# Attention scores from keys and queries split into a rounded part and a rest, three products instead of one fp32 matmul

## The chip, the cores and the metric

One core of a Trainium2 chip runs the whole program. The metric is the device time of one execution in microseconds; lower is better.

## The reference

The program computes an attention layer with a compressive memory, a mixture of experts with hard routing, and a dense mixture of experts with Sinkhorn weights. Only the attention is touched here. Cut to it:

```python
B, H, S, D = 4, 8, 576, 64
scores = (q @ k.T) / sqrt(D)              # causal mask, per batch and head
a = softmax(scores)                       # max taken off, sum + 1e-9
local = a @ v
q_p = where(q > 0, q, exp(q) - 1) + 1     # phi
mem = (q_p @ M_prev) / (q_p . z_prev + 1e-6)
out = g * mem + (1 - g) * local           # g = sigmoid(beta), per head
# out goes, as rows of 512, into the two mixtures of experts
```

All inputs and outputs are fp32.

## The kernel before

The attention works in 16 units (the function `attention`, variable `u`): a unit is one batch and one pair of heads, and the two heads lie in partitions 0 to 63 and 64 to 127 once they are transposed. Per unit the 576 tokens are four tiles of 128 and one of 64.

For unit `u` the kernel loads k, q, v (`load`, on SP's queue), works out phi on ScalarE, GpSimd and VectorE (`phi_a`, `phi_b`, `phi_c`), and transposes k, q and phi on TensorE into PSUM (`trans`, parts 0, 1, 2 for the first 512 tokens, 3 for the last 64 of all). The transposed keys leave PSUM by a VectorE copy (line 204), the queries half by ScalarE (line 206) and half by VectorE (line 207), times 0.125, and phi by ScalarE (line 209, tile `pT`). The last 64 tokens leave by lines 211 to 215.

`score(u, i)` makes the scores of query tile `i` against `w` keys. For `i` from 0 to 3 there is one fp32 matmul for each head, 64 rows deep (line 233), and a bf16 matmul that adds the mask (line 235); then VectorE takes the maximum of both heads (line 237, tile `nm`), and ScalarE the exponentials with their sums, head by head (line 239, tile `P`). Tile 4 holds the last 64 queries of both heads side by side, 128 rows deep, in two matmuls of 288 keys (line 243), with lines 244 to 247 behind it.

`ptrans(u, k)` transposes the probabilities back on TensorE (lines 268, 276, 283, 289) and takes them out of PSUM into `pt`, for `k` in `DVE_PT` on VectorE, else on ScalarE (lines 270, 279); `k` = 6 is shared by both (lines 285, 286). `inverse` transposes the reciprocal sums (lines 173, 174). `av(u, part)` multiplies phi with the memory (line 298, which reads `pT`) and the probabilities with v (line 306) in one PSUM tile, called `x` here, and VectorE scales it into `xT` (line 307). Every fourth unit the router is run on a finished batch (`rt.batch`).

The stage is software-pipelined: the body for `u` runs the scores of unit `u`, the `ptrans` and `av` of unit `u` - 1 and the `trans` of unit `u` + 1, in five steps. The scores come in the order 3, 2, 1, 0, 4; after score 3 come `ptrans` 5 and 4 and `trans` part 0 (keys); after score 2 `ptrans` 0 and 1, `inverse` and part 1 (queries); after score 1 `ptrans` 2 and 3 and part 2 (phi); after score 0 `ptrans` 6 and 7, the first half of `av` and part 3; after score 4 the second half of `av`.

PSUM has two score tiles (`ps_s`, two banks each) and four others of one bank (`ps_t`), which the transposes, the `x` tiles and the router share: a tile is written again only when what reads it is done. Each engine works its own queue in order. The order of each queue in this stage is set when the kernel is built, by a planner that starts from the program's order and takes an instruction that it holds to be ready before one that it doesn't. The two mixtures behind the attention have their order written by hand, and already use matmuls of three products on tiles of type fp32r, split by a ScalarE copy (the rounded part) and a VectorE subtraction (the rest).

Of the kernel before, what the change touches and what calls it, by code (L numbers as in the profile page):

```python
# [9 lines left out]
F32 = mybir.dt.float32  # L10
F32R = mybir.dt.float32r
BF16 = mybir.dt.bfloat16
I32 = mybir.dt.int32
AF = mybir.ActivationFunctionType
ALU = mybir.AluOpType
# [3 lines left out]
B, H, S, D = 4, 8, 576, 64  # L19
# [2 lines left out]
DM = H * D  # L22
NT = 5
DVE_PT = (1, 3, 5)
TW = [128, 128, 128, 128, 64]


def attention(ctx, tc, q, k, v, M_prev, z_prev, beta, xT, ident, router=None):
    nc = tc.nc
    es = ctx  # L30
    c1 = es.enter_context(tc.tile_pool(name="at_c", bufs=1))
    nat = es.enter_context(tc.tile_pool(name="at_nat", bufs=3))
    tmp = es.enter_context(tc.tile_pool(name="at_tmp", bufs=2))
    tr = es.enter_context(tc.tile_pool(name="at_tr", bufs=2))
# [38 lines left out]

    qTp = []
    for i in range(2):
        t = c1.tile([128, 640], F32, name=f"qTp{i}")
        nc.gpsimd.memset(t[:, 512:], 0.0)
        qTp.append(t)
    Mb = []
    for i in range(2):  # L80
        t = c1.tile([128, NP, 128], F32, name=f"Mb{i}")
# [3 lines left out]
    zt, ld, ph, un = {}, {}, {}, {}  # L85

    nrm, Rs = [], []
    for i in range(2):
        t = c1.tile([128, NT, 2], F32, name=f"nrm{i}")
        nc.vector.memset(t, 1.0)  # L90
        nrm.append(t)
        t = c1.tile([128, S], F32, name=f"R{i}")
# [83 lines left out]
    def phi_t(u):  # L176
        if "pT" not in un[u]:
            un[u]["pT"] = tr.tile([128, S], F32, tag="pT", name="pT")
        return un[u]["pT"]

    def trans(u, part):


        qt = qTp[u % 2]
        p = ps_t.tile([128, 512], F32, tag="t", name="tp")
        if part == 0:
            un[u] = {"kT": tr.tile([128, S], F32, tag="kT", name="kT"), "P": {}}
        if part < 3:
            src = (ld.get((u, "k")), ld.get((u, "q")), ph[u][1] if u in ph else None)[part]
            for i in range(4):  # L190
                nc.tensor.transpose(p[:, i * 128:(i + 1) * 128], src[:, i], ident)
        else:
            src = []
            if part == 3:
                src += [ld[u, "k"], ld[u, "q"]]
                if u > 0:
                    src.append(ph[u - 1][1])
            else:
                src += [ph[u][1]]
            for n, t in enumerate(src):  # L200
                nc.tensor.transpose(p[:, n * 64:(n + 1) * 64], t[:64, 4], ident[:64, :64])

        if part == 0:
            nc.vector.tensor_copy(un[u]["kT"][:, :512], p)
        elif part == 1:
            nc.scalar.activation(qt[:, 256:512], p[:, 256:], AF.Copy, scale=0.125)
            nc.vector.tensor_scalar(qt[:, :256], p[:, :256], 0.125, None, ALU.mult)
        elif part == 2:
            nc.scalar.copy(phi_t(u)[:, :512], p)
        elif part == 3:  # L210
            nc.vector.tensor_copy(un[u]["kT"][:, 512:], p[:, 0:64])
            nc.scalar.activation(qt[0:64, 512:576], p[0:64, 64:128], AF.Copy, scale=0.125)
            nc.vector.tensor_scalar(qt[64:128, 576:640], p[64:128, 64:128], 0.125, None, ALU.mult)
            if u > 0:
                nc.vector.tensor_copy(phi_t(u - 1)[:, 512:], p[:, 128:192])
        else:
            nc.vector.tensor_copy(phi_t(u)[:, 512:], p[:, 0:64])

    def score(u, i):

        b, a = divmod(u, NP)
        kT = un[u]["kT"]
        qt = qTp[u % 2]
        s = ps_s.tile([128, 2, 512], F32, tag="s", name="s")
        nm = sm.tile([128, 2], F32, tag="nm", name="nm")
        if i == 3:
            un[u]["su"] = sm.tile([128, NT, 2], F32, tag="su", name="su", bufs=2)
        sums = un[u]["su"][:, i]
        if i < 4:
            w = (i + 1) * 128  # L230
            for h in range(2):
                r = slice(h * 64, (h + 1) * 64)
                nc.tensor.matmul(s[:, h, :w], qt[r, i * 128:(i + 1) * 128], kT[r, :w], start=True, stop=False)
            for h in range(2):
                nc.tensor.matmul(s[:, h, w - 128:w], idb, mk, start=False, stop=True)
            P = pp.tile([128, 2, w], F32, tag=f"P{i}", name=f"P{i}")
            nc.vector.tensor_reduce(nm, s[:, :, :w], AX.X, ALU.max, negate=True)
            for h in range(2):
                nc.scalar.activation(P[:, h], s[:, h, :w], AF.Exp, bias=nm[:, h:h + 1], accum_out=sums[:, h:h + 1])
        else:  # L240
            w = 288
            for h in range(2):
                nc.tensor.matmul(s[:, h, :w], qt[:, 512:640], kT[:, h * w:(h + 1) * w], start=True, stop=(h == 0))
            nc.tensor.matmul(s[:, 1, 224:288], idb, mk2, start=False, stop=True)
            P = pp.tile([128, 2, w], F32, tag=f"P{i}", name=f"P{i}")
            nc.vector.tensor_reduce(nm[:, 0:1], s[:, :, :w], AX.XY, ALU.max, negate=True)
            nc.scalar.activation(P, s[:, :, :w], AF.Exp, bias=nm[:, 0:1], accum_out=sums[:, 0:1])
        un[u]["P"][i] = P
# [8 lines left out]
    def ptrans(u, k):  # L257
# [7 lines left out]
        if k < 4:  # L265
            j, h = divmod(k, 2)
            for i in range(j, 4):
                nc.tensor.transpose(p[:, (i - j) * 128:(i - j + 1) * 128], P[i][:, h, j * 128:(j + 1) * 128], ident)
            ev = nc.vector.tensor_copy if k in DVE_PT else nc.scalar.copy
            ev(pt[:, h, j, j * 128:512], p[:, :512 - j * 128])  # L270
        elif k < 6:
            j = k - 2
            n = 4 - j
            for h in range(2):
                for i in range(j, 4):
                    nc.tensor.transpose(p[:, (h * n + i - j) * 128:(h * n + i - j + 1) * 128],
                                        P[i][:, h, j * 128:(j + 1) * 128], ident)
            ev = nc.vector.tensor_copy if k in DVE_PT else nc.scalar.copy
            ev(pt[:, :, j, j * 128:512], p[:, :2 * n * 128].rearrange("p (h q) -> p h q", h=2))
# [12 lines left out]
    def av(u, part):  # L292
# [7 lines left out]
        for j in range(nj):  # L300
            for h in range(2):
                kk = TW[j]
                lv = vn[:kk, j, h * 64:(h + 1) * 64]
# [13 lines left out]
    for part in (0, 1, 3):  # L317
        trans(0, part)
    phi_a(0)
    for u in range(NU + 1):  # L320
# [9 lines left out]
        for n in range(5):  # L330
            if sc:
                score(u, (3, 2, 1, 0, 4)[n])
                if n == 4:
                    phi_c(u)
            if ex:
                if n == 0:
                    norm(u - 1)
                    ptrans(u - 1, 5)
                    ptrans(u - 1, 4)
                elif n < 3:  # L340
                    ptrans(u - 1, 2 * n - 2)
                    ptrans(u - 1, 2 * n - 1)
                    if n == 1:
                        inverse(u - 1)
                    else:
                        trans(u - 1, 2)
                elif n == 3:
                    ptrans(u - 1, 6)
                    ptrans(u - 1, 7)
                    av(u - 1, 0)  # L350
                else:
                    av(u - 1, 1)
                    if rt and u % NP == 0:
                        rt.batch(u // NP - 1, ps_t)
            if sc:
                if n == 0:
                    phi_b(u)
                elif n == 2:
                    gate_v(u)
                elif n == 3 and u + 1 == NU:  # L360
                    trans(u, 4)
# [290 lines left out]
def tile_attention_moe_moe(ctx, tc, q, k, v, M_prev, z_prev, beta, modality_id, w_gate1, modality_bias, w1a, w2a,  # L652
# [10 lines left out]
    with ExitStack() as actx:  # L663
        xTp = actx.enter_context(tc.tile_pool(name="xTp", bufs=1))
        xT = xTp.tile([128, NP, N], F32, name="xT")
        rt = attention(actx, tc, q, k, v, M_prev, z_prev, beta, xT, ident,
                       lambda: Router(actx, tc, c, xT, ident, modality_id, w_gate1, modality_bias))
        rt.table(rt.ps)
        rt.busy(64)
# [618 lines left out]
```

## Time and profile before

| what | us |
|---|---|
| three runs | 2077.13, 2078.49, 2080.11 (median 2078.49) |
| the profiled execution | 2078.23 |
| its span | 2076.5 |
| busy TensorE, VectorE, ScalarE, GpSimd over the span | 2038.2, 1480.6, 853.7, 776.9 |
| the attention's 16 units, first score to the end of the last unit's scores | about 11 to 266 |

The profile is of one execution. PE is TensorE, PEld its weight loads, DVE VectorE, ACT ScalarE, POOL GpSimd, SP the engine that issues most DMAs. A wait is put down to the instruction that ended it.

### The profile page before, as it was taken

Reading aid. Unit: us, or ns where it says so; the run is one execution under the profiler, and the core shown is the slowest. Engines: PE = TensorE matmul, PEld = TensorE weight load, DVE = VectorE, ACT = ScalarE, POOL = GpSimd, SP = SyncE. Lnnn points to the kernel's source line nnn. Section 1 sums busy time; section 2 is a strip of 40 time slices with the busy share of each in tenths; the row PEclk is TensorE's granted clock in tenths of the full one; section 3 lists DMA queues with packets and bytes.
Section 4 is the critical chain, followed back from the end, with each engine's and each line's share of the span. In section 5 each row is a group of like instructions: output and inputs, shape, how many; then the busy total and the mean of one; then the engine's idle time right before and its main releaser. Section 6 shows DMA issues by size and latency. Waiting matters only on the chain.

```text
span 2076.5 us, 31532 instructions
## 1 busy us (share of the span) xinstructions
PE 2038.2 (98%) x11528; PEld 1768.1 (85%) x11528; DVE 1480.6 (71%) x2573; ACT 853.7 (41%) x1808; POOL 776.9 (37%) x800
## 2 busy tenths in 40 slices
PE   7999999999899999999999999999999999999998
PEld 4666669999698998998888999899888899899987
DVE  6788757666786776667786677777678676677775
ACT  4656536555634333333343333333334433333332
POOL 6666511000133344344454334334355333333332
PEclk9999999999999999999999999999999999999999
DMA  7332146665611233444432222222223222122221
GB/s 189 83 75 78 33 153 229 202 210 170 215 51 61 68 67 69 62 66 77 61 107 67 61 77 66 62 76 67 62 62 111 62 63 80 61 64 79 62 62 40
DMA packets 238520, 187.35 MB, mean 90 GB/s; under 512 B 71440, under 2 KB 194320, under 8 KB 238352
## 3 DMA queue, kind: packets, MB, share of 16 engines
q1 hardware_dynamic: 229008, 171.48, 30.2%
q0 software_dynamic: 3520, 9.46, 1.3%
q10 hardware_dynamic: 5824, 4.25, 0.7%
q8 instruction: 95, 1.56, 0.3%
q14 instruction: 73, 0.60, 0.1%
HBM read 171.51 MB, written 13.64 MB: 89 GB/s over the span
## 4 chain that ended last, share of the span: by engine, by line
PE 46%; issue 16%; POOL 8%; DVE 3%; ACT 1%; POOLq 0%; DVEq 0%; ACTq 0%
PE y L1092 24%; PE prod L1021 21%; POOL T L913 4%; POOL w1l L907 3%; DVE w2l L907 0%; DVE c L1035 0%; DVE u L1035 0%; POOL out_dram L394 0%; DVE hl L1044 0%; PE lq L1133 0%; DVE S2l L907 0%; ACT hh L1039 0%; DVE A11l L907 0%; DVE A12l L907 0%; DVE csum L1166 0%
## 5 line engine op out<-in xcount | busy, mean ns | idle before, releaser
L1039 ACT ACTIVATE hh<-c 128x384 fp32r<-128x384 f32 x384 | 202.0, 526 | 837.3 <-DVE c L1035 837.2
L907 POOL TENSOR_TENSOR w1l<-T,w1h 128x1024 fp32r<-128x1024 f32 x94 | 226.7, 2412 | 851.0 <-ACT w1h L907 851.0
L1092 PE MATMUL y<-w2h,hh 128*128 128x512 f32 x1152 | 453.8, 394 | 0.0
L1092 PE MATMUL y<-w2l,hh 128*128 128x512 f32 x1152 | 453.8, 394 | 0.0
L1092 PE MATMUL y<-w2h,hl 128*128 128x512 f32 x1152 | 453.0, 393 | 0.0
L1044 DVE SCALAR_TENSOR_TENSOR hl<-c,hh 128x384 fp32r<-128x384 f32 x384 | 415.4, 1099 | 1.4 <-ACT hh L1039 1.0
L1035 DVE TENSOR_TENSOR c<-prod,u 128x384 f32<-128x384 f32 x288 | 160.3, 557 | 157.2 <-PE prod L1021 156.7
L1092 PEld LDWEIGHTS y<-w2h,hh 128*128 128x128 f32 x1152 | 216.5, 188 | 32.7
L1092 PEld LDWEIGHTS y<-w2h,hl 128*128 128x128 f32 x1152 | 216.5, 188 | 28.3
L1092 PEld LDWEIGHTS y<-w2l,hh 128*128 128x128 f32 x1152 | 216.7, 188 | 27.8
L913 POOL TENSOR_TENSOR T<-r,T 128x256 f32<-128x256 f32 x188 | 157.8, 840 | 14.1 <-issue 7.0
L913 POOL TENSOR_TENSOR T<-r 128x256 f32<-128x256 f32 x188 | 158.8, 845 | 7.1
L1035 DVE TENSOR_TENSOR u<-prod,u 128x384 f32<-128x384 f32 x192 | 106.0, 552 | 58.3 <-PE prod L1021 58.0
L1035 DVE TENSOR_TENSOR u<-prod,p 128x384 f32<-128x384 f32 x96 | 53.5, 557 | 127.2 <-PE prod L1021 127.1
L907 DVE TENSOR_TENSOR w2l<-r,w2h 128x512 fp32r<-128x512 f32 x188 | 137.1, 729 | 0.5 <-ACT w2h L907 0.5
L907 ACT CAST w2h<-r 128x512 fp32r<-128x512 f32 x188 | 106.7, 610 | 0.0
L907 DVE TENSOR_TENSOR w1l<-r,w1h 128x512 fp32r<-128x512 f32 (+1 forms) x188 | 104.6, 557 | 0.0
L1035 DVE TENSOR_TENSOR c<-prod,p 128x384 f32<-128x384 f32 x96 | 53.4, 557 | 68.8 <-PE prod L1021 64.1
L907 ACT CAST w1h<-T 128x1024 fp32r<-128x1024 f32 x94 | 97.0, 1032 | 1.0 <-POOL T L913 1.0
L1049 ACT COPY p<-prod 128x384 f32<-128x384 f32 x96 | 46.1, 480 | 120.8 <-PE prod L1021 120.6
L1103 DVE SCALAR_TENSOR_TENSOR acc<-y,P,acc 128x512 f32<-128x512 f32 x126 | 92.5, 744 | 4.3 <-PE y L1092 4.3
L907 ACT CAST w1h<-r 128x512 fp32r<-128x512 f32 (+1 forms) x188 | 94.5, 503 | 0.0
(386 smaller groups left out, 4202.9 us busy)
## 6 DMA issues: line engine op xcount, KB each, us to landing
r<-in_moe_w_dram SPq DMA_DIRECT2D x188, 512.0 KB, 4.5
r<-in_moe_w_dram SPq DMA_DIRECT2D x188, 256.0 KB, 2.9
xr<-xs_sorted SPq DMA_DIRECT2D x22, 256.0 KB, 5.1
kn<-in_k_dram SPq DMA_DIRECT2D x32, 128.0 KB, 2.6
qn<-in_q_dram SPq DMA_DIRECT2D x32, 128.0 KB, 2.7
vn<-in_v_dram SPq DMA_DIRECT2D x32, 128.0 KB, 2.8
xs_sorted<-zrow ACTq DMA_DIRECT2D x16, 256.0 KB, 3.1
zb<-in_z_prev_dram SPq DMA_DIRECT2D x4, 256.0 KB, 3.8
```

The costliest lines, as they stand in the source:

```text
L907: return (lambda: nc.scalar.copy(hi, src)), (lambda: eng.tensor_tensor(lo, src, hi.bitcast(F32), ALU.subtract))
L913: sub = lambda i, a, b: (lambda: nc.gpsimd.tensor_tensor(T[:, i], a, b, ALU.subtract))
L1021: nc.tensor.matmul(p, a[:, kd], b[:, kd], start=(i == 0), stop=(i == 5))
L1035: nc.vector.tensor_tensor(st[o], a, st[b], ALU.add)
L1039: nc.scalar.activation(hh[:, f, a * HT:(a + 1) * HT], st[o], AF.Relu)
L1044: nc.vector.scalar_tensor_tensor(hl[:, f, w], st[o], 0.0, hh[:, f, w].bitcast(F32), ALU.max, ALU.subtract)
L1049: nc.scalar.copy(st["p1"], p)
L1092: nc.tensor.matmul(yt[t], a[:, f, t * 128:(t + 1) * 128], b[:, f], start=(j == 0 and f == 0 and i == 0), stop=(j == NJ - 1 and f == 1 and ...
L1103: nc.vector.scalar_tensor_tensor(acc[t], yt[t], P[:, m, e:e + 1], acc[t], ALU.mult, ALU.add)
```

## The change

Keys and queries are now kept as two fp32r tiles each: a rounded part (`kh`, `qh`), which ScalarE writes from PSUM, and a rest (`kl`, `ql`), which VectorE works out from PSUM and the rounded part. Each score is three products that add up in PSUM: rounded by rounded, rounded queries by the rest of the keys, the rest of the queries by rounded keys. In the scores 0 to 3 the two heads alternate within each product.

```diff
+PRODUCTS = ((0, 0), (0, 1), (1, 0))
...
-        t = c1.tile([128, 640], F32, name=f"qTp{i}")
-        nc.gpsimd.memset(t[:, 512:], 0.0)
-        qTp.append(t)
+        qTp.append([c1.tile([128, 640], F32R, name=f"q{n}{i}") for n in "hl"])
+        for t in qTp[-1]:
+            nc.gpsimd.memset(t[:, 512:].bitcast(F32), 0.0)
...
-            un[u] = {"kT": tr.tile([128, S], F32, tag="kT", name="kT"), "P": {}}
+            un[u] = {"kT": [tr.tile([128, S], F32R, tag=f"k{n}", name=f"k{n}T") for n in "hl"], "P": {}}
...
+        kh, kl = un[u]["kT"]
+        qh, ql = qt
+
+        def scaled(r, w, src):
+            nc.scalar.activation(qh[r, w], src, AF.Copy, scale=0.125)
+            nc.vector.scalar_tensor_tensor(ql[r, w], src, 0.125, qh[r, w].bitcast(F32), ALU.mult, ALU.subtract)
+
         if part == 0:
-            nc.vector.tensor_copy(un[u]["kT"][:, :512], p)
+            nc.scalar.copy(kh[:, :512], p)
+            nc.vector.tensor_tensor(kl[:, :512], p, kh[:, :512].bitcast(F32), ALU.subtract)
         elif part == 1:
-            nc.scalar.activation(qt[:, 256:512], p[:, 256:], AF.Copy, scale=0.125)
-            nc.vector.tensor_scalar(qt[:, :256], p[:, :256], 0.125, None, ALU.mult)
+            scaled(slice(0, 128), slice(0, 512), p)
...
-            nc.vector.tensor_copy(un[u]["kT"][:, 512:], p[:, 0:64])
-            nc.scalar.activation(qt[0:64, 512:576], p[0:64, 64:128], AF.Copy, scale=0.125)
-            nc.vector.tensor_scalar(qt[64:128, 576:640], p[64:128, 64:128], 0.125, None, ALU.mult)
+            nc.scalar.copy(kh[:, 512:], p[:, 0:64])
+            nc.vector.tensor_tensor(kl[:, 512:], p[:, 0:64], kh[:, 512:].bitcast(F32), ALU.subtract)
+            for h in range(2):
+                scaled(slice(h * 64, (h + 1) * 64), slice(512 + h * 64, 576 + h * 64), p[h * 64:(h + 1) * 64, 64:128])
...
-            for h in range(2):
-                r = slice(h * 64, (h + 1) * 64)
-                nc.tensor.matmul(s[:, h, :w], qt[r, i * 128:(i + 1) * 128], kT[r, :w], start=True, stop=False)
+            for n, (x, y) in enumerate(PRODUCTS):
+                for h in range(2):
+                    r = slice(h * 64, (h + 1) * 64)
+                    nc.tensor.matmul(s[:, h, :w], qt[x][r, i * 128:(i + 1) * 128], kT[y][r, :w], start=(n == 0), stop=False)
...
-                nc.tensor.matmul(s[:, h, :w], qt[:, 512:640], kT[:, h * w:(h + 1) * w], start=True, stop=(h == 0))
+                for n, (x, y) in enumerate(PRODUCTS):
+                    nc.tensor.matmul(s[:, h, :w], qt[x][:, 512:640], kT[y][:, h * w:(h + 1) * w], start=(n == 0),
+                                     stop=(h == 0 and n == 2))
```

## Rows read from the trace of the kernel before

**Rows 1.** Units by stretch: length; PE, PEld, DVE, ACT, POOL busy (instructions); clock; DMA
```profile
106.94:121.91 14.97, 14.53 (x110) 9.24 (x106) 12.69 (x32) 9.81 (x31) 9.58 (x12) 1.00 0.24 54
121.91:136.26 14.35, 14.33 (x109) 9.26 (x105) 11.89 (x30) 9.00 (x29) 8.69 (x11) 1.00 0.36 83
```

**Rows 2.** Timeline of PE, unit at 121.91: start, length, line, tiles, shapes, count
```profile
121.91 1.13 PE L233 MATMUL s<-kT,qTp 64*128 64x512 f32 x4
122.97 0.29 PE L235 MATMUL s<-mk,idb 128*128 128x128 bf16 x2
...
129.05 0.49 PE L233 MATMUL s<-kT,qTp 64*128 64x128 f32 x4
129.47 0.28 PE L235 MATMUL s<-mk,idb 128*128 128x128 bf16 x2
...
130.34 0.70 PE L298 MATMUL x<-pT,Mb 128*128 128x256 f32 x2
...
132.09 1.24 PE L243 MATMUL s<-kT,qTp 128*128 128x288 f32 x4
133.17 0.19 PE L244 MATMUL s<-mk,idb 128*128 128x64 bf16 x1
```

**Rows 3.** Timeline of ACT in the same unit, idle time and what ended it in brackets
```profile
124.01 0.58 ACT L279 COPY pt<-tp 128x512 f32<-128x512 f32 x1 [1.55 <-PE tp L276]
124.56 0.69 ACT L239 ACTIVATE P<-s,nm 128x512 f32<-128x512 f32 x1
...
127.57 0.58 ACT L174 COPY R<-rp__1669 128x512 f32<-128x512 f32 x1
128.04 0.40 ACT L206 ACTIVATE qTp<-tp 128x256 f32<-128x256 f32 x1
128.39 0.48 ACT L270 COPY pt<-tp 128x384 f32<-128x384 f32 x1
...
129.70 0.59 ACT L209 COPY pT<-tp 128x512 f32<-128x512 f32 x1
```

**Rows 4.** Timelines of ACT and PE in the unit at 106.94
```profile
110.35 0.69 ACT L239 ACTIVATE P<-s,nm 128x512 f32<-128x512 f32 x1 [0.72 <-DVE nm L237]
...
115.28 0.65 ACT L209 COPY pT<-tp 128x512 f32<-128x512 f32 x1
...
115.98 0.70 PE L298 MATMUL x<-pT,Mb 128*128 128x256 f32 x2
```

**Rows 5.** Waits from 60 to 266: who waited for whom, us in total, times, longest
```profile
PEld x L298 <- ACT pT L209: 4.6, 13, 0.8
```

**Rows 6.** The chain of waits in the dense experts: start, length, fp32r products of 384, 512 columns
```profile
576.41 1.04 PE prod L1021 x6
577.45 1.15 PE y L1092 x5
```

**Rows 7.** Timeline of DVE, unit at 121.91
```profile
124.77 0.68 DVE L204 COPY kT<-tp 128x512 f32<-128x512 f32 x1
125.46 0.96 DVE L237 TENSOR_REDUCE nm<-s 128x2 f32<-128x768 f32 x1
...
128.06 0.69 DVE L237 TENSOR_REDUCE nm<-s 128x2 f32<-128x512 f32 x1 [1.03 <-PE s L235]
128.67 0.41 DVE L207 TENSOR_SCALAR qTp<-tp 128x256 f32<-128x256 f32 x1
...
130.80 0.76 DVE L128 SCALAR_TENSOR_TENSOR qp<-ex,qp 128x512 f32<-128x512 f32 x1 [1.25 <-POOL qp L127]
...
134.21 0.23 DVE L213 TENSOR_SCALAR qTp<-tp 64x64 f32<-64x64 f32 x1
```

**Rows 8.** Groups by line, 0 to 620 us: name, shapes, count | busy, mean ns | idle before
```profile
L676 DVE TENSOR_TENSOR xl<-xtp,xh 128x512 fp32r<-128x512 f32 x20 | 13.7, 690 | 14.2 <-ACT xh L675 14.0
```

**Rows 9.** Timeline of PE in the unit at 40.59
```profile
51.28 1.14 PE L243 MATMUL s<-kT,qTp 128*128 128x288 f32 x4
52.25 0.59 PE L298 MATMUL x<-pT,Mb 128*128 128x256 f32 x2
```

## The prediction

> **What bounds the kernel now.** I read the page first, then the busy time by stretch, unit by unit through the attention, then the timelines of TensorE, ScalarE and VectorE in one steady unit, and last the list of waits. The page gives TensorE 98% of the span. In a steady unit it is the same: 14.33 of 14.35 us busy at a granted clock of 1.00, with VectorE at 11.89 and ScalarE at 9.00 [rows 1]. Read so, every TensorE nanosecond saved would count.
>
> The timelines say something else. From 124.01 to 130.29 ScalarE has no idle time: it starts when TensorE hands it the fourth `ptrans` (line 279) and ends with `pT` (line 209, 129.70 + 0.59) [rows 3]. The first `av` matmul, line 298, reads `pT` and starts at 130.34, 0.05 after [rows 2, 3]. It waits for `pT` in 13 units, 4.6 us in all [rows 5]. So in a unit there are two paths that end almost together at line 298: TensorE's own work, and ScalarE's stretch. The unit at 106.94 shows what a later ScalarE does. There the first exponential waits 0.72 us for VectorE's maximum and starts 3.41 us into the unit, against 2.65 in the unit at 121.91 (124.56 - 121.91); `pT` ends at 8.99 against 8.38, line 298 starts at 9.04 against 8.43, and the unit lasts 14.97 us against 14.35 [rows 1 to 4]. Some 0.6 us late on ScalarE became 0.6 us of unit, with TensorE in the same order.
>
> **The change part by part.**
>
> *The products.* Score 3 takes 1.06 us up to its mask (121.91 to 122.97) and score 0 0.42 us (129.05 to 129.47) [rows 2]. Four matmul instructions of 512 or of 128 columns stand in them, the heads side by side, so the difference of 0.64 us over 384 columns is 1.67 ns a column, and 0.42 - 0.213 = 0.207 us is left for the first weights and the turn to the full array. I keep this constant. An fp32r product takes 1.15 / 5 = 0.230 us at 512 columns and 1.04 / 6 = 0.173 at 384 [rows 6]; the line through both gives 0.116 at 256 and 0.131 at 288. With the heads side by side, as now:
> score 3: 0.207 + 3 x 0.230 = 0.90 for 1.06, -0.16;
> score 2: 0.207 + 3 x 0.173 = 0.73 for 0.207 + 384 x 0.00167 = 0.85, -0.12;
> score 1: 0.207 + 3 x 0.116 = 0.56 for 0.63, -0.07;
> score 4: four instructions in 1.08 us (132.09 to 133.17) become six, 0.11 + 6 x 0.131 = 0.90 (0.11 being half the constant), -0.18.
> No row has fp32r at 128 columns. The line gives 0.06 a product, score 0 then takes 0.39; a product that cost a whole fp32 matmul of 128 columns (0.213) would make it 0.85. I take 0.52, +0.10, nearer to the fp32r rows; the ends are -0.03 and +0.43. Sum on TensorE: -0.43 us a unit, with the ends -0.56 and -0.10.
>
> *The keys' and queries' way out of PSUM.* Both rounded parts are ScalarE's now and both fall into the stretch that ends with `pT`. `kh` is a copy of 128x512 out of PSUM, as line 174: 0.58 us. `qh` is the same size in place of line 206's 0.40: +0.18. That is +0.76 us by lengths; by distances from start to start (0.47 for line 174, 0.35 for line 206) it is +0.59 [rows 3]. The stretch starts earlier by what score 3 saves, 0.16. So `pT`, and with it line 298, come 0.76 - 0.16 = 0.60 us later in the unit (0.43 by the shorter measure). TensorE would get there 0.16 + 0.12 + 0.07 - 0.10 = 0.25 us sooner and waits. Behind line 298 only score 4 gets shorter: -0.18. Net +0.42 us a unit, or +0.25. The uncertain score 0 is hidden in the wait.
>
> *VectorE.* `kl` (0.69 by the like subtraction [rows 8]) replaces a copy of 0.68 [rows 7]: nothing. `ql` replaces 0.41 by some 0.7: +0.3. Of the last 64 tokens it gets one more small instruction: +0.23. Its 2.28 us idle in the unit (1.03 + 1.25) [rows 7] cover +0.5 of work. What they may not cover is waiting: `kl`, `ql` and the three small rests each wait in VectorE's queue for a ScalarE instruction, and the maxima, `pt` copies and `x` scalings queue behind them. If the planner fills these waits they cost nothing; if not, three small ones of about 0.2 [rows 7] on the way to the next maximum, less 0.3 to be filled, cost 0.3 a unit. I count 0 and keep 0.3 for the range.
>
> The Trainium skill ("Perfetto Trace Analysis", section Identifying the Most-Contended Engine) says that TensorE's matmul occupancy is a bad measure of its nearness to its limit, that weight-load occupancy is a better one, and that plain occupancy is fair for VectorE and ScalarE. The trace fits: weight loads are 9.26 of 14.35 us, 65%, and VectorE's 11.89 is 83% [rows 1]. By the page VectorE, to which the change adds work, would be the engine to watch; that is the second rival below.
>
> *The rest.* Two more GpSimd memsets at the start and the added weight loads lie beside other work or inside the sums above. DMAs, SP's queue and everything behind the attention are the same instructions; they move with its end, since the router's table, from which the experts' loads take their addresses, comes after it.
>
> **Sum.** Units 2 to 14, 13 of them, prepare a next unit and have line 298 behind `pT` [rows 5]; the first two, and the last, which splits nothing, I count at 0, with +-1 us. 13 x 0.42 = +5.5 us. The profiled execution's own time is 2078.23 (span 2076.5 and 1.73 around it), which is 0.26 under the median of the runs. Forecast: 2078.2 + 5.5 = 2083.7. Its own range: 13 x 0.25 = 3.3 gives 2081.5; 13 x (0.42 + 0.3) = 9.4 gives 2087.6.
>
> **The rivals.**
>
> *1. TensorE stays the bound: faster.* The planner may see that `pT` is late and put score 4 ahead of line 298, as it did in the unit at 40.59, where line 243 runs at 51.28 and line 298 at 52.25 [rows 9]. Score 4's 0.9 us fill the 0.85 us of wait (0.60 + 0.25), and the saving of 0.43 counts in 16 units: -6.9, 2071.3; with score 0 at its dear end, 16 x 0.10 = 1.6, 2076.6. For it: that row. Against it: in the unit at 106.94, with `pT` late as well, the order was not changed [rows 4].
>
> *2. VectorE becomes the bound: much slower.* The maximum of score 3 and the transposed keys are ready at nearly the same time. If `kh` is queued behind the two exponentials (2 x 0.69 [rows 3]), VectorE gets `kl` only after 1.38 + 0.58 us, of which the next maximum (0.96) and a small copy (0.23, as line 213's [rows 7]) fill 1.19: a wait of 0.77. VectorE then has 11.9 + 0.5 of work, its 2.3 of idle time, whose causes stay, and 0.77: 15.45 us a unit, +1.1. 13 x 1.1 = 14.3: 2092.5. It decides once VectorE's work and waits pass TensorE's 13.9. For it: the program's order has the exponentials first. Against it: the planner goes by what is ready.
>
> *3. The two effects cancel.* If only the three small transposes of part 3 (0.33 us) move ahead of line 298, the unit is 0.42 - 0.33 = 0.1 longer: 13 x 0.1 = 1.3, 2079.5, and with parts of rival 1 anything from 2075 to 2082.
>
> *4. The change doesn't do what it says: the heads no longer run side by side.* Then six products stand where three do: score 3 0.207 + 6 x 0.230 = 1.59 (+0.53), score 2 +0.40, score 1 +0.27, score 0 +0.5, score 4 -0.18, together +1.5 a unit, 16 x 1.5 = 24: 2102. Against it: the heads alternate in the new loop, and differ in partitions and banks as before.
>
> **How the numbers follow.** Forecast 0.35, rival 1 0.27, rival 2 0.15, rival 3 0.18, rival 4 0.05. About 0.2%, 4.2 us, is what a measurement of this kernel can tell from no change: faster is under 2074.3, slower over 2082.7. Of rival 1 0.22 is faster, 0.05 same. Rival 3 is same, and of the forecast 0.06, its low end. Slower: 0.29 + 0.15 + 0.05 = 0.49. Faster 0.22, same 0.29. The range 2071 to 2092 leaves out half of rival 2, rival 4 and the low part of rival 1, some 0.2 in all.
>
> **What would show it.** Steady units of about 14.8 us; ScalarE without idle time from line 279's to line 209's work, some 0.7 us longer; line 298 waiting for `pT` 0.5 us or more a unit, with TensorE's busy time lower in them. Score 3 at 0.90 us to its mask, score 4 at 0.90 show the products; score 0 at 0.85 shows their dear end. Units of 13.9 us with score 4 ahead of line 298 are rival 1; VectorE idle before `kl`, and the score 3 maximum late, rival 2; a score 3 of 1.6 us rival 4. The forecast is wrong if line 298 doesn't wait.

## The result and the profile after

| | kernel before | with the change |
|---|---|---|
| median | 2078.92 us (4 runs, 2077.13 to 2080.11) | 2092.62 us (4 runs, 2089.91 to 2093.71) |
| ratio | | 1.0065, 95% interval 1.0047 to 1.0082 |
| profiled execution, its span | 2078.23, 2076.5 | 2091.93, 2090.2 |
| steady unit | 14.35 | 15.41 |
| start of unit 3, of unit 15 | 57.0, 252.8 | 63.5, 267.5 |

Slower by 13.7 us, where +5.5 was forecast. The steady unit is that of units 7 and 11; the other kinds stand in the second table of the experiments. A unit is counted here from its first score 3 product to the next unit's. The span grew by 13.7 too, in two places of nearly the same size: the first three units end 6.5 us later (63.48 for 57.01), and the twelve from unit 3 to unit 14 take 204.07 us for 195.82, +8.25. All the rest is 1.0 us shorter.

Two stretches of the changed kernel (length; PE, PEld, DVE, ACT, POOL busy; granted clock; DMA), unit 2 and a steady unit, which answers to [rows 1]:

```profile
40.58:63.48 22.90, 19.27 (x120) 13.29 (x117) 11.50 (x30) 11.59 (x36) 9.69 (x11) 0.78 0.53 156
...
199.56:214.97 15.41, 14.26 (x119) 9.97 (x115) 11.69 (x31) 10.03 (x31) 8.79 (x10) 1.00 0.26 59
```

The steady unit grew by 1.06 us and TensorE lost 0.07 of its busy time: the whole growth is waiting. TensorE in this unit (start, length, line, tiles, shapes, count, idle time before and what ended it), for [rows 2]; lines 310, 254 and 256 are lines 298, 243 and 244 of before:

```profile
199.56 0.51 PE L243 MATMUL s<-khT,qh 64*128 64x512 f32 x2
...
200.47 0.28 PE L245 MATMUL s<-mk,idb 128*128 128x128 bf16 x2
...
206.72 0.33 PE L243 MATMUL s<-khT,qh 64*128 64x128 f32 x2
...
207.21 0.28 PE L245 MATMUL s<-mk,idb 128*128 128x128 bf16 x2
...
207.77 0.27 PE L301 MATMUL tp<-ident,P 128*64 128x128 f32 x1
208.34 0.70 PE L310 MATMUL x<-pT,Mb 128*128 128x256 f32 x2 [0.30 <-ACT pT L217]
...
210.10 0.41 PE L254 MATMUL s<-khT,qh 128*128 128x288 f32 x1
...
211.02 0.20 PE L256 MATMUL s<-mk,idb 128*128 128x64 bf16 x1
211.88 0.81 PE L310 MATMUL x<-pT,Mb 128*128 128x320 f32 x2 [0.66 <-DVE pt L302]
```

Up to the first `av` the unit is late by `pT`, as forecast, and by less: 8.78 us for 8.43, +0.35 for +0.60. Score 4 wins its 0.16 and ends at 211.22. Then the second `av` waits 0.66 us, for VectorE. That wait is the step that the prediction did not have. VectorE's queue ahead of it:

```profile
209.36 0.41 DVE L247 TENSOR_REDUCE nm<-s 128x2 f32<-128x256 f32 x1
210.62 0.69 DVE L150 TENSOR_REDUCE nrm<-ex 128x8 f32<-128x512 f32 x1 [0.86 <-POOL ex L132]
211.23 0.41 DVE L297 COPY pt<-tp 128x256 f32<-128x256 f32 x1
211.56 0.27 DVE L302 COPY pt<-tp 64x128 f32<-64x128 f32 x1
```

The two copies of the transposed exponentials (lines 297 and 302) free the PSUM tile that the second `av` writes. TensorE finished their transposes by 208.04 (the last one is at 207.77), yet they come at 211.23: ahead of them in the queue stands `phi_b`'s reduction of line 150, for which VectorE idles 0.86 us until GpSimd has its operand. Before, in the unit at 121.91, both follow the maximum at once, and the reduction (line 149) comes behind them:

```profile
131.48 0.41 DVE L237 TENSOR_REDUCE nm<-s 128x2 f32<-128x256 f32 x1
131.82 0.41 DVE L285 COPY pt<-tp 128x256 f32<-128x256 f32 x1
132.15 0.27 DVE L290 COPY pt<-tp 64x128 f32<-64x128 f32 x1
...
133.53 0.67 DVE L149 TENSOR_REDUCE nrm<-ex 128x8 f32<-128x512 f32 x1
```

The reduction is ahead of the last copy in nine of the twelve units 3 to 14 of the changed kernel (not in 5, 9 and 13, behind a change of batch), and in none of them before. Grouped from 70 to 266 us (us in total, times, longest), the weight loads of the `av` matmuls wait as follows; the second line answers to [rows 5]:

```profile
PEld x L310 <- DVE pt L302: 8.9, 12, 0.8
...
PEld x L310 <- ACT pT L217: 5.7, 12, 0.6
```

Before, from 60 to 266 us, the first of these waits was rare:

```profile
PEld x L298 <- DVE pt L290: 1.5, 3, 0.6
```

ScalarE, for [rows 3]: without idle time from line 291 (279 before) to `pT` (line 217), and `kh` (line 212) is ahead of the exponentials:

```profile
201.50 0.59 ACT L291 COPY pt<-tp 128x512 f32<-128x512 f32 x1 [2.36 <-PE tp L288]
201.99 0.59 ACT L212 CAST khT<-tp 128x512 fp32r<-128x512 f32 x1
202.47 0.70 ACT L249 ACTIVATE P<-s,nm 128x512 f32<-128x512 f32 x1
...
205.86 0.66 ACT L208 ACTIVATE qh<-tp 128x512 fp32r<-128x512 f32 x1
...
207.62 0.67 ACT L217 COPY pT<-tp 128x512 f32<-128x512 f32 x1
```

The early loss is in unit 2. ScalarE's queue also issues the DMAs that write zeros for the experts (line 488). Here seven stand in a row ahead of unit 2's first exponential:

```profile
41.14 6.20 ACTq L488 DMA_DIRECT2D xs_sorted<-zrow  x7
47.45 0.69 ACT L249 ACTIVATE P<-s,nm 128x512 f32<-128x512 f32 x1 [6.67 <-DMA xs_sorted<-zrow]
```

Before there are five, and that exponential waits 5.42 us, until 45.83:

```profile
40.50 5.22 ACTq L476 DMA_DIRECT2D xs_sorted<-zrow  x5
45.83 0.69 ACT L239 ACTIVATE P<-s,nm 128x512 f32<-128x512 f32 x1 [5.42 <-DMA xs_sorted<-zrow]
```

In the changed kernel TensorE then idles 2.76 us (to 48.95, for `P`), and the granted clock is at half, 1.2 GHz, for the next ten us, where it was 1.00 over unit 2 before (the last line):

```profile
48.95 0.39 PE L243 MATMUL s<-khT,qh 64*128 64x256 f32 x2 [2.76 <-ACT P L249]
```

```profile
49.20:59.40 10.20, 10.20 (x48) 7.31 (x46) 3.89 (x10) 7.08 (x22) 3.59 (x4) 0.50 0.06 23
40.59:57.01 16.42, 14.78 (x109) 9.29 (x105) 11.71 (x28) 9.47 (x30) 10.45 (x12) 1.00 0.65 178
```

### The profile page after: what moved, and what is told of

It is laid out like the page before. It is cut to its first block, busy times and chain, and to the rows that moved or that the text cites. A ratio compares the mean times of both kernels' runs of the same rounds, so it can differ in the third digit from the quotient of the medians.

```text
span 2090.2 us, 31909 instructions
## 1 busy us (share of the span) xinstructions
PE 2041.6 (98%) x11688; PEld 1784.0 (85%) x11688; DVE 1478.3 (71%) x2589; ACT 871.5 (42%) x1856; POOL 777.2 (37%) x802
## 4 chain that ended last, share of the span: by engine, by line
PE 45%; issue 16%; POOL 8%; DVE 3%; ACT 0%; POOLq 0%; ACTq 0%; DVEq 0%
PE y L1104 24%; PE prod L1033 21%; POOL T L925 4%; POOL w1l L919 3%; DVE w2l L919 0%; DVE u L1047 0%; DVE c L1047 0%; POOL out_dram L406 0%; DVE hl L1056 0%; DVE S2l L919 0%; DVE A11l L919 0%; DVE A12l L919 0%; PE lq L1145 0%; DVE csum L1178 0%; PE lg L1157 0%
## 5 line engine op out<-in xcount | busy, mean ns | idle before, releaser
L925 POOL TENSOR_TENSOR T<-r,T 128x256 f32<-128x256 f32 x188 | 157.0, 835 | 13.9 <-issue 6.8
L1047 DVE TENSOR_TENSOR u<-prod,u 128x384 f32<-128x384 f32 x192 | 106.0, 552 | 59.1 <-PE prod L1033 58.8
```

The source lines that it names most:

```text
L925: sub = lambda i, a, b: (lambda: nc.gpsimd.tensor_tensor(T[:, i], a, b, ALU.subtract))
L1047: nc.vector.tensor_tensor(st[o], a, st[b], ALU.add)
```

## The experiments

Theory A: the loss is two queue orders, the reduction ahead of the copies on VectorE and the zero DMAs on ScalarE; the split itself costs little. Its rivals: the split's own work costs it (on ScalarE or VectorE), or the products do. Each ratio is to runs of the kernel before on the same chip (their median: 2078.92 for the change, 2080.95 to 2081.59 for the rest), so ratios are compared; 0.001 is 2.1 us.

| kernel | median | ratio, 95% interval | steady unit | unit 3 starts |
|---|---|---|---|---|
| change | 2092.62 | 1.0065 (1.0047 to 1.0082) | 15.41 | 63.5 |
| e1_order | 2087.39 | 1.0028 (1.0019 to 1.0038) | 14.52 | 64.6 |
| e2_clear_sp | 2090.90 | 1.0041 (1.0029 to 1.0054) | 15.41 | 56.0 |
| e3_split_fp32 | 2088.69 | 1.0033 (1.0021 to 1.0046) | 14.87 | 61.5 |
| e4_one_product | 2075.10 | 0.9965 (0.9951 to 0.9979) | 13.16 | 60.2 |
| e5_kh_dve | 2084.77 | 1.0021 (1.0011 to 1.0031) | 14.37 | 61.3 |
| e6_order_clear | 2080.97 | 1.0002 (0.9992 to 1.0011) | 14.52 | 55.2 |
| e7_order_clear_swap | 2101.29 | 1.0096 (1.0079 to 1.0113) | 14.7 to 15.4 | 60.3 |
| e8_before_clear_swap | 2096.02 | 1.0070 (1.0051 to 1.0090) | 14.85 | 58.8 |
| e9_swap_pin | 2084.74 | 1.0018 (1.0009 to 1.0027) | 13.95 | 56.8 |
| e10_order_clear_kh | 2078.59 | 0.9985 (0.9976 to 0.9994) | 14.38 | 55.2 |
| e11_swap_pin_kh | 2086.70 | 1.0031 (1.0021 to 1.0041) | 13.95 to 15.0 | 55.0 |
| e12_before_clear | 2076.21 | 0.9979 (0.9969 to 0.9988) | 14.36 | 52.2 |
| e13_pin_batch | 2068.98 | 0.9938 (0.9924 to 0.9952) | 13.95 | 53.7 |
| e14_swap_but_batch | 2075.16 | 0.9964 (0.9950 to 0.9977) | 13.95 | 55.0 |
| e15_before_pin_batch | 2065.19 | 0.9920 (0.9906 to 0.9933) | 14.07 | 53.6 |

The units are of several kinds, and 1.06 us is the growth of the steady ones (7 and 11). Units 3 to 14 in the profiles, in us:

| units | before | change | e1_order | e13_pin_batch | e15_before_pin_batch |
|---|---|---|---|---|---|
| 3 | 14.36 | 15.35 | 14.70 | 13.95 | 14.07 |
| 7, 11 | 14.35 | 15.41 | 14.52 | 13.95, 13.97 | 14.07 |
| 6, 10, 14 | 14.97 to 15.03 | 15.40, 15.41 | 14.52 | 13.94 to 14.00 | 14.43 to 14.91 |
| 4, 8, 12 | 16.92 to 17.14 | 17.10 to 17.31 | 16.50 to 16.72 | 15.59 to 15.80 | 15.71 to 15.93 |
| 5, 9, 13, behind a change of batch | 18.34 to 19.82 | 19.93 to 20.17 | 19.95 to 21.13 | 19.19 to 20.34 | 18.38 to 19.97 |
| 3 to 14 together | 195.82 | 204.07 | 198.72 | 189.77 | 190.36 |

In the diffs below, `...` marks what is cut, and `NoSync` is short for the full form of the dependency, an order without a wait.

**e1_order.** A rule of order, without a wait: `phi_b`'s two reductions don't go ahead of the last transposes' copy of the unit that is being finished.

```diff
+        for i in reds if u - 2 in last else ():
+            tc.add_manual_dep(i.ins, last[u - 2].ins.name, NoSync, reason="order on VectorE")
...
+            last[u] = nc.vector.tensor_copy(un[u]["pt4"], ...)
```

> The changed kernel, with one rule added for VectorE's queue alone: the two reductions of phi_b may not stand ahead of the copies of ptrans 7 that are written earlier in the program. Theory A (a reduction that waits for GpSimd stands in VectorE's queue ahead of the copies that free the PSUM tile for the second half of av): the wait of 0.85 us before that half goes, steady units fall from 15.4 to about 14.6 us, and 11 to 13 units give 9 to 11 us: about 2082. Theory B (VectorE has too much work and handover waits, wherever they stand): the idle time turns up at another place, steady units stay at 15.2 to 15.4, 2090 to 2093.

Steady unit 14.52, as theory A said; its time, 2082, was missed. VectorE and TensorE in the steady unit:

```profile
207.02 0.41 DVE L252 TENSOR_REDUCE nm<-s 128x2 f32<-128x256 f32 x1
207.35 0.40 DVE L302 COPY pt<-tp 128x256 f32<-128x256 f32 x1
207.69 0.27 DVE L307 COPY pt<-tp 64x128 f32<-64x128 f32 x1
208.29 0.69 DVE L151 TENSOR_REDUCE nrm<-ex 128x8 f32<-128x512 f32 x1 [0.33 <-POOL ex L133]
```
```profile
206.00 0.70 PE L315 MATMUL x<-pT,Mb 128*128 128x256 f32 x2 [0.29 <-ACT pT L222]
...
208.69 0.79 PE L315 MATMUL x<-pT,Mb 128*128 128x320 f32 x2
```

The first `av` still waits 0.29 for `pT` (8.76 into the unit, which began at 197.24), the second has no wait. So in a steady unit 0.89 of the 1.06 us is the reduction's place, and 0.17 is what ScalarE's longer stretch costs net. Over units 3 to 14 the rule takes 5.35 us of the 8.25: nothing is gained in units 5, 9 and 13, where the reduction was not ahead. The 2.9 us left are 4.8 lost in those three units, less 1.9 gained in the others together. No run isolates what waits in the three units with e1's rule. The first units are as slow as with the change. By the ratio the run gains 7.7 us, of the 9 to 11 expected. In the kernel before the rule would find nothing to change in units 3 to 14.

**e2_clear_sp.** The zero DMAs are issued from SP's queue.

```diff
-                nc.scalar.dma_start(self.xs[...], z)
+                nc.sync.dma_start(self.xs[...], z)
```

> The changed kernel, with the 16 DMAs that write zeros issued from SP's queue instead of ScalarE's. Theory A (the first three units lose some 6.5 us because seven of these DMAs stand in a row in ScalarE's queue, TensorE runs out of work behind them and its clock falls to half for 10 us): the third unit falls from 22.9 to about 16, unit 3 starts near 57 instead of 63.5, steady units stay at 15.4: about 2086. Theory B (the slow start comes from the added handovers of the first unit): unit 3 starts within 1.5 us of 63.5, about 2092.

Unit 2 takes a steady unit's time, at full clock:

```profile
40.58:56.00 15.42, 14.25 (x119) 9.95 (x115) 11.54 (x29) 9.36 (x30) 8.90 (x11) 1.00 0.83 284
```

Unit 3 starts 7.5 us sooner; the ratio falls by 0.0024, 5 us, where theory A had 6.6 (2086). In the profile the dense experts' products (`prod`) start 2.5 us sooner than in the changed kernel (565.3 for 567.8) and end together with its own: the granted clock between the attention and `prod` is 0.94 for 0.97. Part of the gain was given back behind the attention.

**e6_order_clear.** Both edits.

> Both mended orders at once: phi_b's two reductions stay behind the last transposes' copies (e1_order), and the zero DMAs are issued from SP's queue (e2_clear_sp). Theory A: the gains add up; the first three units end near 56 us, the steady unit is 14.5, and the run is within 3 us of the kernel before. Theory B (something behind the attention became slower with the change, or gives the gain back): the run stays 5 us or more above the kernel before, though the attention is no longer late.

Theory A's values: unit 3 at 55.2, 14.52, and the kernel before's time. The drops of 0.0037 and 0.0024 make 0.0061 together, and 0.0063 was measured. The two orders explain the loss against the kernel before, which itself has the zero DMAs in ScalarE's queue (see e12_before_clear).

**e3_split_fp32.** The change's split, every instruction of it, but the scores are one fp32 matmul of the rounded parts (the rests go unused).

```diff
-PRODUCTS = ((0, 0), (0, 1), (1, 0))
+PRODUCTS = ((0, 0),)
...
+                    nc.tensor.matmul(s[:, h, :w], qt[x][r, ...].bitcast(F32), kT[y][r, :w].bitcast(F32), ...)
```

> All of the split (rounded parts by ScalarE, rests by VectorE), but the scores are one fp32 matmul on the rounded parts alone; the rests are written and left out of the scores. Theory A (the split's work on ScalarE and VectorE sets the unit, the products only shorten waits): at least as slow as the changed kernel, steady units 15.4 to 15.8, 2092 to 2098. Theory B (the fp32r products themselves, or the alternation of heads, cost more than fp32): back near 2079, steady units near 14.4.

14.87: neither theory's number. Theory A took the order on VectorE for the split's doing; but here the copies come ahead of the reduction, and what remains is `pT` (VectorE, then TensorE):

```profile
205.00 0.41 DVE L297 COPY pt<-tp 128x256 f32<-128x256 f32 x1
205.33 0.27 DVE L302 COPY pt<-tp 64x128 f32<-64x128 f32 x1
...
207.04 0.67 DVE L150 TENSOR_REDUCE nrm<-ex 128x8 f32<-128x512 f32 x1
```
```profile
204.17 0.70 PE L310 MATMUL x<-pT,Mb 128*128 128x256 f32 x2 [0.35 <-ACT pT L217]
```

The split alone costs 0.52 us in a steady unit, by ScalarE's stretch: the first `av` comes at 8.94 for 8.43. The bad order comes only with the three products: the order on VectorE changes with the matmuls, though VectorE's instructions are the same.

**e4_one_product.** Only the first product; the two with the rests are left out.

```diff
-PRODUCTS = ((0, 0), (0, 1), (1, 0))
+PRODUCTS = ((0, 0),)
```

> The changed kernel with only the first of the three products (the other two are left out, the rests are still written). It takes some 1.7 us of TensorE work out of each unit. Theory A (ScalarE's stretch and VectorE's queue set the unit): steady units fall by no more than 0.7, to 14.7 to 15.4, 2083 to 2092. Theory B (TensorE sets it): steady units near 13.7 and 16 x 1.7 = 27 us less, about 2065.

Both missed: 13.16, and 2075.10 us. The order is yet another, with score 4 and the copies early. It shows that the split's work on ScalarE and VectorE does not hold a unit at 14.4 or more where TensorE has less to do.

**e5_kh_dve.** e1_order with the rounded keys copied by VectorE.

```diff
-            nc.scalar.copy(kh[:, :512], p)
+            nc.vector.tensor_copy(kh[:, :512], p)
```

> e1_order with one more move: the rounded keys of the first 512 tokens are written by a VectorE copy in place of the ScalarE copy. That takes 0.48 us (start to start) out of ScalarE's stretch from line 291 to pT. Theory A (pT on ScalarE sets the first av, and so the unit): the first av comes about 8.3 us into the unit in place of 8.76, the steady unit goes from 14.5 to about 14.1, and the run is some 5 us under e1_order. Theory B (VectorE, which takes 0.7 us more, sets the unit): the unit stays at 14.5 or grows, and the run gains nothing or loses.

14.37, a gain of 0.15 of the 0.4 that theory A gave: the first `av` comes at 8.60 in place of 8.76, still behind `pT`, because VectorE's next maximum, for which ScalarE's next exponentials wait, comes 0.36 us later in the unit (4.02 for 3.66 in e6). **e10_order_clear_kh** is e6_order_clear with the same edit.

> e6_order_clear with the rounded keys written by VectorE, as in e5_kh_dve. If gains add up: steady unit 14.37 as there, first units as in e6_order_clear, some 2 us under e6_order_clear (2081), so 2078.5 to 2079.5. If the 0.15 us per unit is given back at the changes of batch (units 5 and 9, where e5 had 19.1 and 23.8): the same as e6_order_clear or above.

2078.59, as said. **e12_before_clear** is the kernel before with e2's edit alone.

> A control: the kernel before with the zero DMAs issued from SP's queue, nothing else. Its steady units stay at 14.35, its third unit goes from 16.4 to some 14.4, so about 2 us faster than the kernel before. e6_order_clear less this kernel is what the split and the products cost where neither the zero DMAs nor the order on VectorE is in the way: 13 units of 14.52 less 14.35, +2 us. If this kernel is no faster than before, what the zero DMAs cost in the first units is given back later.

It is faster than before by 0.0021 +- 0.0010 (4 us for the 2 expected). Against it the split and the products still cost 0.0023 (e6) or 0.0006 (e10, inside the intervals). In the profiles most of e6's loss lies ahead of unit 3, which starts at 55.2 for 52.2; units 3 to 14 take 198.77 us for 198.12. In unit 0 the granted clock is 0.52 from 9.47 to 25.37 in e6, and 0.77 from 12.57 to 22.40 in e12. Neither order accounts for these 3 us, and no run isolates them; with the moves of e13 and e15 unit 3 starts at 53.7 and 53.6.

**e7_order_clear_swap, e8_before_clear_swap.** e6, and the kernel before with e2's edit, with phi's transposes ahead of the reciprocal-sum transposes in the program.

```diff
                     if n == 1:
-                        inverse(u - 1)
+                        trans(u - 1, 2)
                     else:
-                        trans(u - 1, 2)
+                        inverse(u - 1)
```

> e6_order_clear, with phi's transposes put ahead of the reciprocal-sum transposes in the program (right behind score 2), so that their turn on ScalarE and VectorE comes earlier. Theory A: the stretch that ends in pT gets shorter, TensorE's own work sets the unit, 13.7 to 13.9 us; about 8 us under e6_order_clear, and 6 to 8 us under the kernel before. Theory B (pT still last, or another wait takes its place): 14.3 or more, and no more than 3 us of gain on e6_order_clear.

> A control: the kernel before, with its fp32 score products and no split, and with the two moves of e7_order_clear_swap (zero DMAs from SP's queue, phi's transposes ahead of the reciprocal-sum transposes). Steady unit about 14.1 us, the run 2 to 4 us faster than the kernel before. Its difference from e7_order_clear_swap is what the products and the split are worth where neither waits: by the shorter products 0.3 to 0.45 us per unit, 4 to 7 us in favour of e7. If this kernel is as fast as e7, the three products are worth nothing on their own.

Both expectations failed, and both kernels became slower: with `pT` early, the product on `qp` (line 130) goes ahead of the maximum of score 1 on VectorE and waits for GpSimd there (1.74 us in e7's unit of 15.40, 1.0 to 1.3 in its shorter ones), and TensorE waits for the maximum's followers. With these moves too the change is 5 us behind the kernel without it; e7 has e1's rule besides, and e8 has not.

**e9_swap_pin.** e7 with that product held behind the maximum; **e11_swap_pin_kh** is e9 with e5's edit.

```diff
-            nc.vector.scalar_tensor_tensor(p, e, 1.0, p, ALU.min, ALU.add)
+            i = nc.vector.scalar_tensor_tensor(p, e, 1.0, p, ALU.min, ALU.add)
+            if u - 1 in mx:                    # mx: the maximum of score 1
+                tc.add_manual_dep(i.ins, mx[u - 1].ins.name, NoSync, reason="order on VectorE")
```

> e7_order_clear_swap, with the product on qp (line 130) held behind the maximum of score 1 on VectorE, where it stood in e6_order_clear; in e7 it went ahead of that maximum and waited 1.74 us for GpSimd. Theory A (that one place in VectorE's queue was what e7 lost by, and phi's transposes done early do shorten ScalarE's stretch): the steady unit goes from 14.7-15.4 to 13.7-13.9, the run to 2070-2075, under both kernels. Theory B (phi's transposes done early push the tail of ScalarE's or VectorE's work late, whatever the place of that product): the unit stays at 14.3 or more, the run at 2080 or more.

> e9_swap_pin with the rounded keys written by VectorE. If ScalarE's stretch no longer ends last there (Theory A of e9), this gains nothing: within 2 us of e9_swap_pin, or above by what VectorE's 0.7 us adds per unit. If pT or another of ScalarE's results still ends last, it gains 0.15 us or more per unit, 2 us or more.

The unit is 13.95, near theory A's 13.7 to 13.9, and the run is not near its 2070 to 2075: the units behind a change of batch (5, 9, 13) take 24.3 to 25.3 us, where e6 has 20.2 to 21.2. Here is unit 5 of e9 on VectorE, then on TensorE, then the clock right after:

```profile
100.17 0.77 DVE L130 SCALAR_TENSOR_TENSOR qp<-ex,qp 128x512 f32<-128x512 f32 x1 [2.58 <-POOL qp L129]
100.86 0.68 DVE L218 SCALAR_TENSOR_TENSOR ql<-tp,qh 128x512 fp32r<-128x512 f32 x1
```
```profile
101.69 1.09 PE L306 MATMUL tp<-ident,P 128*128 128x128 f32 x4 [2.63 <-DVE ql L218]
```
```profile
101.00:107.80 6.80, 6.11 (x26) 4.49 (x27) 4.32 (x15) 2.55 (x10) 3.00 (x4) 0.50 0.14 32
```

In those units GpSimd is late with its part (line 129), VectorE's queue stands behind it for 2.58 us, TensorE waits 2.63 us, and then runs at half clock. e11 gains nothing on e9, as said for the case that ScalarE's stretch no longer ends last, and has the same long units.

**e13_pin_batch, e14_swap_but_batch.** In units 5, 9 and 13 (and in unit 1, which has no change of batch ahead) the product is held behind the last transposes' copies (e13), or phi's transposes keep their old place (e14).

```diff
+            at = last.get(u - 2) if u % NP == 2 else mx.get(u - 1)      # e13
...
+                    if (n == 1) == (u % NP != 1):                        # e14
```

> e9_swap_pin, and in the units behind a change of batch (5, 9, 13) the product on qp (line 130), which there waits for GpSimd, is held behind the copies of the last transposes on VectorE. Theory A (that wait on VectorE is what starved TensorE for 2.6 us and halved its clock there): steady units stay at 13.95, the three units go from 24.3-25.3 back to 20 or less, the run is 10 to 14 us under e9_swap_pin, 2070 to 2075, faster than the kernel before. Theory B (the early transposes of phi delay something else at the change of batch): the three units stay above 23 and the run at 2080 or more.

> e9_swap_pin, but in the units behind a change of batch (5, 9, 13) phi's transposes come behind the reciprocal-sum transposes again, as in e6_order_clear. By theory A of e13 and by its theory B alike these units go back to the 20.2 to 21.2 us of e6_order_clear; steady units 13.95. Some 10 us under e9_swap_pin: 2073 to 2077. If the units stay above 23, neither the wait for GpSimd nor the transposes' place there is the cause.

e13 has these units at 19.5, 20.3 and 19.2 and is 12.6 us faster than the kernel before, a little better than theory A said. e14 has 19.9, 22.8 and 20.9, the second above its 20.2 to 21.2, and half of that gain, inside its expected time.

**e15_before_pin_batch.** The kernel before with every move of e13: what are the products worth?

> A control: the kernel before, fp32 products and no split, with every move of e13_pin_batch. If the shorter products are worth their 0.43 us per unit: steady unit 14.35, where TensorE has no wait left, and the run 4 to 6 us slower than e13_pin_batch. If the moves alone make the gain: steady unit 13.95 and the same time as e13_pin_batch. Its unit can't be shorter than TensorE's own work in one, some 14.2 us by e8_before_clear_swap's trace less its waits there.

A miss, and the fastest kernel of all by its median. Its steady unit (the first fence) is TensorE's own work, without any wait, and below the 14.2 that was given as its least; then come the transposes ahead of score 0:

```profile
181.33:195.40 14.07, 14.07 (x110) 9.26 (x106) 11.18 (x29) 9.22 (x28) 8.75 (x11) 1.00 0.29 65
```
```profile
187.28 0.83 PE L280 MATMUL tp<-ident,P 128*128 128x128 f32 x6
187.94 0.60 PE L183 MATMUL rp__2557<-ident,rr 128*128 128x128 f32 x4
```

And e13's steady unit, with the same transposes, the first weight load of line 184 with its wait, and ScalarE's copy that it waits for:

```profile
102.79:116.73 13.94, 13.85 (x119) 9.88 (x115) 12.17 (x34) 10.65 (x33) 9.90 (x13) 1.00 0.25 58
```
```profile
108.36 0.82 PE L292 MATMUL tp<-ident,P 128*128 128x128 f32 x6
109.28 0.66 PE L184 MATMUL rp__1687<-ident,rr 128*128 128x128 f32 x4
```
```profile
109.28 0.42 PEld L184 LDWEIGHTS rp__1687<-ident,rr 128*128 128x128 f32 x4 [0.33 <-ACT pT L227]
```
```profile
108.61 0.62 ACT L227 COPY pT<-tp 128x512 f32<-128x512 f32 x1
```

From the first of these transposes to line 184's it is 0.92 us in e13 and 0.66 in e15: 0.26 us a unit is spent waiting until `pT` has left its PSUM tile (109.23), on a ScalarE that has the rounded parts to write. Without it e13's unit would be 13.68; by this estimate the products are worth 0.39 us, of which 0.13 reaches the unit. Units 3 to 14 take 189.8 us for 190.4: e13 gains in every kind of unit but 5, 9 and 13, where it loses 0.4 to 0.9 us each.

e15 still ends 3.8 us earlier (0.0018; the intervals overlap by 0.0009). In the two profiles the experts behind the attention start within 0.9 us of each other (e13 sooner) and reach 493.1 together; then e13 loses 3.9 us up to `prod`, where its granted clock is lower:

```profile
493.10:548.70 55.60, 46.23 (x348) 41.33 (x346) 36.00 (x61) 33.48 (x74) 0.00 (x0) 0.89 0.68 224
```
```profile
493.10:544.80 51.70, 43.23 (x347) 39.73 (x345) 34.32 (x60) 33.10 (x74) 0.00 (x0) 0.96 0.66 219
```

The first line is e13's. Over all five runs its mean clock is 0.992 to 0.993, and e15's 0.994 to 0.996, so the lower clock is not confined to one profile; where in the span it is lower in the other runs, no trace shows. Why the clock falls more in a stretch whose instructions did not change stays open, and with it why e15 ends earlier: from unit 3 to unit 14 of the attention e13 is the faster one.

## Why the prediction was wrong

Its direction was right and its size was not; 2092.62 lies just above the range.

*The products* were right: score 3 0.91 (forecast 0.90), score 2 0.73 (0.73), score 1 0.54 (0.56), score 0 0.49 (0.52), score 4 0.92 (0.90). That is -0.46 us of TensorE a unit for the -0.43 forecast (score 1 was 0.64 before, where the working had 0.63), and the estimate from e13 and e15 is 0.39. The heads run side by side: rival 4 is out.

*ScalarE's stretch* was the right mechanism, a little oversized. It runs from 201.50 to 208.29, 6.79 us for 6.28: +0.51, where +0.76 was used and +0.59 was the shorter measure. It starts 0.16 sooner, as said, so the first `av` is 0.35 late, for 0.60. With score 4's -0.16 the net is +0.19, and e1_order shows +0.17 in a steady unit. The term should have been 0.17 x 13 = 2.2 us, in place of 5.5. That one number stood for 13 units was a flaw of its own: e1_order's units 3 to 14 are 2.9 us longer than before's, near the 2.2 by luck, as units 5, 9 and 13 lose 1.3 to 2.2 us each and units 4, 6, 8, 10, 12 and 14 gain 0.4 to 0.5.

*The step that failed is VectorE's*: "If the planner fills these waits they cost nothing; [...] I count 0 and keep 0.3 for the range." The order on VectorE cost 0.89 us in a steady unit and 5.35 us over units 3 to 14, by none of the waits listed there. Not a new instruction but an old one, the reduction of line 150, moved ahead of the copies and waited there for GpSimd. The price that I had bounded was that of the new work; e3_split_fp32 has all of that work and not the wait. The order in the queue was taken as given, and it changes with the matmuls, as e3, e4 and the change show with three different orders.

*The second step that failed* is "the first two, and the last [...] I count at 0, with +-1 us". Units 0 to 2 cost 6.5 us. The zero DMAs stood in ScalarE's queue before, too, held its exponentials for 5.42 us and made the unit at 40.59 16.42 us long; I read that unit for its order of score 4 [rows 9] and not for its wait. With two more DMAs in the row TensorE idled 2.76 us, and half clock followed. Unit 0, also counted at nothing, ran long too: unit 1 starts 3.1 us later than before (25.41 for 22.30), which a wait of 2.80 us in unit 1 of before hides here, and which shows as 3.0 us between e6 and e12.

*The rivals.* Of the kernels with the split only e4 has rival 1's order (score 4 first) in steady units; the change has it in unit 2 alone. Nor did rival 3's order come: the small transposes of part 3 start at 209.77, behind the first `av` at 208.34. Rival 2 named VectorE and 2092.5, which is the measured time, but not for its reason: `kh` is ahead of the exponentials, at 201.99, and `kl` waits 0.27. VectorE did not become the bound either: it was 11.69 us busy in a unit of 15.41. The Trainium skill ("Perfetto Trace Analysis", section Identifying the Most-Contended Engine) takes plain occupancy as a fair measure of how close VectorE is to its limit. Here that measure fell from 83% to 76% while TensorE began to wait for VectorE. The trace agrees that VectorE was not at its limit, and shows what occupancy leaves out: an engine that idles with its queue blocked looks free.

## What to carry to other kernels

Where an order on the engines is worked out from instruction lengths, a change of the matmuls can be a change of order on another engine: look, for each in-order queue, for an instruction that waits for a slow third engine, and ask what would stand behind it if it moved one place up. Price that, not only the added work; here it was 0.89 us of 1.06 in a steady unit, and one rule of order took it away. Price each kind of unit, too: here the steady ones were 2 of 12. And give the kernel before the same cure before crediting the change: the moves were worth 16.4 us to it (2081.59 to 2065.19), and the three products, some 0.39 us cheaper a unit, left 0.6 us over units 3 to 14 and none in the run.

## What the runs showed of the hardware

An fp32r product of 64 rows costs little at 128 columns: score 0, six of them in pairs, takes 0.49 us up to its mask, against 0.42 for the two heads' fp32 matmuls. Idle times of TensorE of 2.6 to 2.8 us were followed by half clock, 1.2 GHz, for quite different times: 10.2 us after 2.76 in unit 2 of the change, some 6 us after 2.63 in e9's unit 5, and 3.0 us (27.11 to 30.10, granted clock 0.50) after 2.80 in unit 1 of the kernel before. In e9, where waits of 2.3 to 3.3 us came three times a run, the waits and the half clock together took back more than the shorter units had gained: units 3 to 14 take 204.6 us, for 198.8 in e6.
